# Reading the spectrum of h into both partition halves: one load with an outer dimension of two, or two loads of 64 rows

## The chip, the cores and the metric

The kernel runs on one core of one Trainium2 chip. The metric is device time in microseconds (us) of one execution; lower is better.

Names in the profile: PE is TensorE, PEld its weight loads, DVE is VectorE, ACT is ScalarE, POOL is GpSimd, SP is SyncE (which only issues transfers here). L307 is line 307 of the kernel. The change removes two lines, so line 307 of before is line 305 of after.

## The reference

Two layers in a row. The first, which matters here, is a long convolution by FFT:

```python
batch, seq, d_model = (8, 5696, 128)
L = 2 * S
Xf = np.fft.rfft(x, n=L, axis=1)        # x: 8 x 5696 x 128
Hf = np.fft.rfft(h, n=L, axis=0)        # h: 5696 x 128
Yf = Xf * Hf[None, :, :]
y = np.fft.irfft(Yf, n=L, axis=1)[:, :S, :]
# ... then a second layer: phases of y, two 5696 x 5696 token-mixing matrices, a channel mix
```

The second layer takes the last 1800 us and is not touched.

## The kernel before

The convolution is a two-level FFT done with matrix products. It works in eight groups: four pairs of batches times two halves of the channels. For each group there are four stages: A (first level), B (second level and the product with the spectrum of h), C and D (back). In stage B, TensorE makes a chunk of the spectrum of x in PSUM (`f2`); the 128 partitions are 64 rows of real parts and then 64 rows of imaginary parts. ScalarE copies the chunk to `xs`. VectorE multiplies `xs` twice, by the real and the imaginary plane of the spectrum of h. Both partition halves are multiplied by the same 64 rows, so the 64 rows of `hf_hbm[dh, c]` must be present twice, in partitions 0 to 63 and 64 to 127.

```python
fh = pool("fft_h", 4, conv, side="right")          # four buffers for hs
# ... cut ...
hf_hbm = nc.dram_tensor("hf_hbm", (2, 2 * NCK, N2, 2, HD * CK), F16, kind="Internal").ap()   # N2 = 64
# ... cut: h_chunk stores the spectrum of h, 24 stores ...
def stage_b(a_of, dh):
    def chunk(c):
        kh, c0, ck = CHK[c]
        hs = fh.tile([P, 2, HD * CK], F16, tag="hs", name="hs")
        hv = hs.rearrange("p r (d k) -> p r d k", k=CK)
        src = hf_hbm[dh, c]
        nc.sync.dma_start(hs.rearrange("p r n -> p (r n)"),
                          bass.AP(tensor=src.tensor, offset=src.offset,
                                  ap=[[0, 2], [2 * HD * CK, N2], [1, 2 * HD * CK]]))
        ps = f2(a_of, c)                                                   # TensorE
        xs = fs.tile([P, 2, HD, CK], F16, tag="xs", name="xs")
        nc.scalar.activation(xs[:, :, :, :ck], ps, AF.Copy)                # L304
        k0 = HALF[kh][0] + c0
        for r in range(2):
            nc.vector.tensor_tensor(                                       # L307
                uv[r][:, :, :, k0:k0 + ck], xs[:, :, :, :ck],
                hv[:, r:r + 1, :, :ck].to_broadcast([P, 2, HD, ck]), op=mult)
    return [lambda c=c: chunk(c) for c in range(2 * NCK)]                  # 12 chunks
# ... cut: stage C reads all of u_t and v_t (one buffer each) at L322 and L323 ...
    woven(stage_c(st), nxt, now)                     # stage C of this group, stage A of the next
    if dh == 0 and bp + 1 < B // 2:
        x16s[bp + 1] = load_x(bp + 1)                # 2.9 MB input load, by GpSimd, every second group
    # ... cut ...
    woven(stage_b(a_of, groups[g + 1][1]) if nxt else [], stage_d(st, bp, dh), now)
    # stage D ends with two stores of yt (712 KB each), on SyncE's queue like the hs loads
```

An hs load is 128 rows of 2 KB, 256 KB in all. The source pattern is written as "twice (step 0), 64 rows, 1024 elements".

Of the kernel before, what the change touches and what calls it, by code (L numbers as in the profile page):

```python
# [22 lines left out]
def kernel(  # L23
# [10 lines left out]
    nc = tc.nc  # L34
# [50 lines left out]
    N2 = 64  # L85
# [3 lines left out]
    CK = 8  # L89
    HD = D // 2  # L90
# [8 lines left out]
    hf_hbm = nc.dram_tensor("hf_hbm", (2, 2 * NCK, N2, 2, HD * CK), F16, kind="Internal").ap()  # L99
# [25 lines left out]
    for p0, p1 in ((0, 80), (80, NB)):  # L125
        nc.gpsimd.dma_start(u_t[p0:p1, :N2 * D],
                            bass.AP(tensor=h.tensor, offset=h.offset + p0 * N2 * D,
                                    ap=[[N2 * D, p1 - p0], [1, N2 * D]]))
# [79 lines left out]
    def f2(a_of, c):  # L208

        kh, c0, ck = CHK[c]  # L210
        a_, (k0, kn) = a_of[kh], HALF[kh]
        ps = psum()
        for j in range(ck):
            for ri in range(2):
                for e in range(2):
                    rows = slice(64 * e, 64 * e + 64)
                    nc.tensor.matmul(ps[:, e, j * HD:(j + 1) * HD],  # L217
                                     w_t2[rows, k0 + c0 + j, N2 * (1 - ri):N2 * (3 - ri)],
                                     a_[rows, ri * kn + c0 + j, :],
                                     start=(ri == 0), stop=(ri == 1))  # L220
        return ps[:, :, :ck * HD].rearrange("p e (k d) -> p e d k", k=ck)
# [70 lines left out]
    def stage_b(a_of, dh):  # L292

        def chunk(c):
            kh, c0, ck = CHK[c]
            hs = fh.tile([P, 2, HD * CK], F16, tag="hs", name="hs")
            hv = hs.rearrange("p r (d k) -> p r d k", k=CK)
            src = hf_hbm[dh, c]
            nc.sync.dma_start(hs.rearrange("p r n -> p (r n)"),
                              bass.AP(tensor=src.tensor, offset=src.offset,  # L300
                                      ap=[[0, 2], [2 * HD * CK, N2], [1, 2 * HD * CK]]))
            ps = f2(a_of, c)
            xs = fs.tile([P, 2, HD, CK], F16, tag="xs", name="xs")
            nc.scalar.activation(xs[:, :, :, :ck], ps, AF.Copy)  # L304
# [5 lines that stand above are left out]
        return [lambda c=c: chunk(c) for c in range(2 * NCK)]  # L310
# [211 lines left out]
    with tc.tile_pool(name="bpool", bufs=1, reuse_waits="tile") as bp, \  # L522
# [216 lines left out]
        for i, (k, p, tt, j0, s0, nj) in enumerate(stretches):  # L739
# [21 lines left out]
            if tt is None:  # L761
# [17 lines left out]
                if end_of_pair:  # L779
# [5 lines left out]
                    for h in range(2):  # L785
                        c, c0 = cs[h]
# [88 lines left out]
```

## Time and profile before

| | before |
|---|---|
| median time | 2571.7 us (2 runs) |
| span of the profiled run | 2567.6 us |
| eight stages B (end of one stage C to the first matmul of the next) | 53.3, 62.3, 50.2, 62.2, 49.4, 62.0, 49.5, 53.8; sum 442.7 us |
| eight stages C with A | sum 248.0 us |
| end of the last stage C to the end | 1801.2 us |

The 62 us stages are those beside an input load. The first is woven with the making of a table, and the last runs beside a load of 2.9 MB for the next part.

The waits view, lines chosen. Each line says who waited for whom: us in total, how many times, the longest.

```profile
engine line waited for: us in total, times, longest us
...
DVE u_t L307 <- DMA hs<-hf_hbm: 290.3, 64, 16.3
...
ACT xs L304 <- DVE v_t L307: 219.0, 51, 15.8
PEld L322 <- DVE u_t L307: 192.0, 8, 29.5
PE ps L322 <- DVE u_t L307: 190.8, 8, 29.3
```

Read it from the top as a chain: VectorE waits for hs, ScalarE waits for VectorE to free `xs`, TensorE waits (once per group, up to 29 us) for the last product before stage C can start. They are one wait seen three times, so they must not be added.

The timeline of a steady piece of a stage without an input load: start, duration, engine and line; in brackets, the idle time before and who ended it.

```profile
start us, us, engine line op out<-in xcount [idle before <-releaser]
272.81 20.66 SPq L299 DMA_DIRECT2D hs<-hf_hbm  x4
276.17 0.69 DVE L307 TENSOR_TENSOR u_t<-xs,hs 128x1024 f16<-128x1024 f16 x1 [4.25 <-DMA hs<-hf_hbm]
276.78 0.69 DVE L307 TENSOR_TENSOR v_t<-xs,hs 128x1024 f16<-128x1024 f16 x1
...
281.44 0.69 DVE L307 TENSOR_TENSOR u_t<-xs,hs 128x1024 f16<-128x1024 f16 x1 [3.98 <-DMA hs<-hf_hbm]
282.05 0.68 DVE L307 TENSOR_TENSOR v_t<-xs,hs 128x1024 f16<-128x1024 f16 x1
...
286.71 0.69 DVE L307 TENSOR_TENSOR u_t<-xs,hs 128x1024 f16<-128x1024 f16 x1 [3.98 <-DMA hs<-hf_hbm]
```

The products come 5.27 us apart (286.71 - 281.44), 1.3 us of work and 4 us of waiting. A period of 5.27 us for 256 KB is 50 GB/s. And SyncE is busy for 20.66 us with four issues: it is held back too. The tile view of hs gives all its loads of before: shortest, median and longest issue in ns, then the first and last start.

```profile
L299 SPq DMA_DIRECT2D hs<-hf_hbm x96: 482/5082/14242, 37.2 to 714.8; - x96
```

The first six issues, which come 1.2 to 23.7 us apart, take 0.52 to 0.62 us each; the 5.1 us are of issues that follow one another at once. So 5.1 us is not what such an issue costs by itself.

Three stretches with their busy times per engine: the stage B from 253.5 to 303.7 us (no input load), one beside an input load, and everything after the convolution.

```profile
core 0: us, PE busy (x) PEld busy (x) DVE busy (x) ACT busy (x) POOL busy (x), PEclk, DMA share, GB/s
...
159.80:222.10 62.30, 15.70 (x499) 14.43 (x497) 15.81 (x25) 17.07 (x20) 2.17 (x4) 0.62 0.33 83
253.50:303.70 50.20, 15.72 (x498) 14.47 (x496) 16.06 (x25) 17.06 (x20) 0.00 (x0) 0.63 0.13 46
...
766.50:2567.60 1801.10, 1684.78 (x8800) 807.59 (x8798) 1337.32 (x2590) 356.75 (x583) 793.97 (x1464) 0.96 0.83 157
```

In 50 us no engine works for more than 17.1 us, and the sixteen DMA engines together are 13% busy: 2 of 16 is 12.5%. The time hangs on a transfer, and the transfers use little of what there is.

### The profile page before, as it was taken

How to read it: one execution, taken by the hardware profiler on the slowest of the kernel's cores; microseconds unless marked ns; L12 is line 12 of the kernel's file. 1: busy time of each engine (PE TensorE's matmuls, PEld its weight loads, DVE VectorE, ACT ScalarE, POOL GpSimd, SP SyncE). 2: the span in 40 equal slices, each digit the busy share in tenths (PEclk: the TensorE clock that was granted, in tenths of full speed). 3: DMA queues.
4: the chain of work that ended last, by engine and by line, in shares of the span. 5: the costliest groups of instructions: out<-in, count | busy, mean ns of one | idle time of the engine just before them, and what ended most of it. 6: DMA issues, size and time to landing. Idle time of an engine off the chain costs nothing.

```text
span 2567.6 us, 42483 instructions
## 1 busy us (share of the span) xinstructions
PE 2090.9 (81%) x16255; PEld 1197.2 (47%) x16255; DVE 1695.1 (66%) x3004; ACT 637.8 (25%) x931; POOL 841.8 (33%) x1521
## 2 busy tenths in 40 slices
PE   4365446535745669999999999979999999999998
PEld 4365446525743424444444444433444444444444
DVE  5444435524563588888878876778777777777774
ACT  5432333324334522333323300000111111111111
POOL 3200000000002025444454566524445544455441
PEclk9687678767776689999999999999999999999998
DMA  5132231231338589999988999896778877888773
GB/s 119 51 74 62 69 76 61 69 97 42 103 97 197 158 228 171 177 172 174 171 149 166 174 174 143 137 267 109 138 138 153 144 135 138 140 153 138 139 135 66
DMA packets 406108, 340.45 MB, mean 133 GB/s; under 512 B 80879, under 2 KB 363375, under 8 KB 404079
## 3 DMA queue, kind: packets, MB, share of 16 engines
q0 software_dynamic: 218240, 143.00, 41.2%
q1 hardware_dynamic: 180560, 179.40, 23.5%
q10 hardware_dynamic: 7104, 15.34, 1.7%
q8 instruction: 127, 2.08, 0.3%
q14 instruction: 77, 0.63, 0.1%
HBM read 382.55 MB, written 97.93 MB: 187 GB/s over the span
## 4 chain that ended last, share of the span: by engine, by line
PE 55%; DMA 5%; DVE 3%; POOL 2%; issue 1%; ACT 1%; SPq 0%; DVEq 0%; ACTq 0%; POOLq 0%
PE m L814 50%; DMA wb<-in_moe_w_tok_r_dram 2%; POOL wb L536 1%; DMA wb<-in_moe_w_tok_i_dram 1%; DVE c L821 1%; PE utp L626 1%; PE v L633 1%; PE m L775 1%; PE m L777 1%; PE m L818 1%; DMA zr_hbm<-mag 1%; DVE wt L545 1%; DMA y_hbm<-yb 1%; PE theta_ps L377 0%; PE tpz L575 0%
## 5 line engine op out<-in xcount | busy, mean ns | idle before, releaser
L536 POOL DMA_DIRECT2D wb<-in_moe_w_tok_i_dram x720 | 390.0, 553 | 810.8 <-DVE wt L545 732.1
L536 POOL DMA_DIRECT2D wb<-in_moe_w_tok_r_dram x720 | 389.1, 555 | 397.8 <-DMA zr_hbm<-mag 277.3
L814 PE MATMUL m<-b,wt 128*128 128x512 bf16 x1936 | 455.1, 381 | 19.1 <-DVE wt L545 15.0
L545 DVE STREAM_TRANSPOSE wt<-wb 128x384 f32<-128x384 f32 (+2 forms) x720 | 360.1, 523 | 126.3 <-PE m L814 68.0
L814 PEld LDWEIGHTS <-wt 128*128 128x128 bf16 x1936 | 189.5, 98 | 254.3 <-DVE wt L545 18.2
L322 PE MATMUL ps<-r_u,u_t 128*128 128x128 f16 x1024 | 142.4, 231 | 191.7 <-DVE u_t L307 190.8
L821 DVE TENSOR_TENSOR c<-c,m 128x512 f32<-128x512 f32 x440 | 283.3, 669 | 0.0
L307 DVE TENSOR_TENSOR u_t<-xs,hs 128x1024 f16<-128x1024 f16 x96 | 64.2, 669 | 305.9 <-DMA hs<-hf_hbm 290.3
L628 ACT ACTIVATE uts<-utp 128x512 bf16<-128x512 bf16 (+1 forms) x90 | 53.3, 592 | 616.6 <-PE utp L626 616.6
L322 PEld LDWEIGHTS <-u_t 128*128 128x128 f16 x1024 | 111.5, 109 | 192.0 <-DVE u_t L307 192.0
L304 ACT ACTIVATE xs<-ps 128x1024 f16<-128x1024 f32 x96 | 92.1, 979 | 223.0 <-DVE v_t L307 219.0
L135 POOL DMA_DIRECT2D x<-in_x_dram x16 | 8.6, 542 | 419.3 <-PE ps L201 419.0
L201 PE MATMUL ps<-f_t,x 89*128 89x88 f16 (+1 forms) x1024 | 144.9, 302 | 0.8 <-DVE v_t L246 0.8
L323 PE MATMUL ps<-r_v,v_t 128*128 128x128 f16 x1024 | 139.7, 230 | 0.2
L201 PEld LDWEIGHTS <-x 89*128 89x128 f16 x1024 | 136.8, 269 | 1.1 <-issue 0.8
L623 ACT ACTIVATE ub<-c 128x512 bf16<-128x512 f32 (+1 forms) x90 | 56.4, 628 | 226.4 <-DMA wb<-in_moe_w_tok_i_dram 163.2
L323 PEld LDWEIGHTS <-v_t 128*128 128x128 f16 x1024 | 107.5, 105 | 3.0 <-issue 1.7
L217 PEld LDWEIGHTS <-w_t 64*128 64x128 f16 x3240 | 69.0, 108 | 72.7 <-issue 49.5
L577 ACT ACTIVATE yb<-tpz 128x512 bf16<-128x512 bf16 (+1 forms) x46 | 27.5, 597 | 168.5 <-PE tpz L575 132.2
L635 DVE SCALAR_TENSOR_TENSOR c<-v,c 128x512 f32<-128x512 f32 (+1 forms) x90 | 61.4, 682 | 10.8 <-PE v L633 8.6
L379 ACT ACTIVATE red<-theta_ps,magic 128x512 f32<-128x512 f32 (+1 forms) x46 | 31.6, 687 | 136.3 <-PE theta_ps L377 108.8
L307 DVE TENSOR_TENSOR v_t<-xs,hs 128x1024 f16<-128x1024 f16 x96 | 64.8, 675 | 0.0
(2848 smaller groups left out, 3845.3 us busy)
## 6 DMA issues: line engine op xcount, KB each, us to landing
wb<-in_moe_w_tok_r_dram POOLq DMA_DIRECT2D x352, 96.0 KB, 4.5
wb<-in_moe_w_tok_i_dram POOLq DMA_DIRECT2D x352, 96.0 KB, 4.9
wb<-in_moe_w_tok_r_dram POOLq DMA_DIRECT2D x352, 80.0 KB, 4.5
wb<-in_moe_w_tok_i_dram POOLq DMA_DIRECT2D x352, 80.0 KB, 3.9
hs<-hf_hbm SPq DMA_DIRECT2D x96, 256.0 KB
cp_hbm<-c SPq DMA_DIRECT2D x88, 256.0 KB
c<-cp_hbm SPq DMA_DIRECT2D x88, 256.0 KB
out_dram<-c SPq DMA_DIRECT2D x88, 256.0 KB
```

What stands on the lines that cost most here:

```text
L201: nc.tensor.matmul(ps[:, i // 4, (i % 4) * 2 * kn:(i % 4 + 1) * 2 * kn], lhs(q + i), f1_t[:NB, 2 * k0:2 * k0 + 2 * kn], start=True, stop=True)
L217: nc.tensor.matmul(ps[:, e, j * HD:(j + 1) * HD], w_t2[rows, k0 + c0 + j, N2 * (1 - ri):N2 * (3 - ri)], a_[rows, ri * kn + c0 + j, :], sta ...
L304: nc.scalar.activation(xs[:, :, :, :ck], ps, AF.Copy)
L307: nc.vector.tensor_tensor(uv[r][:, :, :, k0:k0 + ck], xs[:, :, :, :ck], hv[:, r:r + 1, :, :ck].to_broadcast([P, 2, HD, ck]), op=mult)
L322: nc.tensor.matmul(o, u_t[:, at:at + P], r_u, start=True, stop=False)
L323: nc.tensor.matmul(o, v_t[:, at:at + P], r_v, start=False, stop=True)
L536: nc.gpsimd.dma_start(wb[32 * i:32 * i + 32, :ng, :nj * 64], bass.AP(tensor=a.tensor, offset=a.offset + row0 * S + p * H + i * QR + j0 * 6 ...
L545: nc.vector.transpose(wt.rearrange("p j t r -> p (j t r)").bitcast(F32).rearrange("p (j g t) -> p g j t", j=TJ, g=4)[:, :ng, :nj], wb[:, : ...
L623: nc.scalar.activation(ub[:m].rearrange("p b d -> p (b d)"), c[:m], AF.Copy)
L635: nc.vector.scalar_tensor_tensor(c[:m], v[:m], 0.0, c[:m], op0=ALU.max, op1=ALU.add)
L814: nc.tensor.matmul(ms[q], a[q][:, j, :, r], bts[jj][q][:, r, :], start=(jj == 0 and r == 0), stop=(jj == NJ - 1 and r == 1 and q not in left))
L821: nc.vector.tensor_tensor(c, z, ms[q], op=op)
```

## The change

Each half is loaded by its own transfer. The bytes moved and the size of the rows stay. The intent is to get rid of the outer dimension of two.

```diff
-            src = hf_hbm[dh, c]
-            nc.sync.dma_start(hs.rearrange("p r n -> p (r n)"),
-                              bass.AP(tensor=src.tensor, offset=src.offset,
-                                      ap=[[0, 2], [2 * HD * CK, N2], [1, 2 * HD * CK]]))
+            for e in range(2):
+                nc.sync.dma_start(hs[64 * e:64 * e + 64], hf_hbm[dh, c])
```

## The prediction

> **What bounds it now.** The change touches only the convolution, the first ~790 of 2567.6 us. There stage B (multiply by the spectrum of h) runs eight times, between stages C+A. By the timeline (end of one stage C to the start of the next) the eight take about 53, 62, 50, 62, 50, 62, 50 and 54 us, 443 together. The waits view: VectorE waits 290.3 us for the hs load at L307, ScalarE 219 us for VectorE, TensorE 191 us at L322 for u_t (eight waits). Stage C needs all of u_t and v_t, one buffer each, so this is critical.
>
> In steady state a multiplication follows the last by 5.27 us, about 4 us of it waiting. 256 KB in 5.27 us is 50 GB/s. The packet records show hs packets of 2048 B, 85 ns each, about 25 per microsecond: two engines' worth of 16. SyncE's queue has 15824 four-byte completion packets; its 977 other transfers at 16 each leave 192 for the 96 hs loads: two each. The Trainium skill, "DMA: Bandwidth & Descriptors", section "Why a DMA increments its semaphore by 16 and not by 1", says why: the engine count is the largest up to 16 that divides the slowest dimension of both sides, here 2. SyncE is held 5.1 us per hs issue (median).
>
> **What the change does.** Same bytes and packets, 192 issues for 96, outermost dimension 64, so 16 engines. Estimate: 8 packets per engine x 85 ns = 0.7 us per chunk, four chunks prefetched. SyncE: 2 x ~0.5 us per chunk (64-row issues of L414 take 0.45 to 0.59 us). The page's "Rules for kernel authors" advises against splitting a transfer into partition halves, since halves share the engines; here the unsplit form has only two engines, so I expect that advice not to hold.
>
> **What then bounds stage B.** The first four chunks, prefetched today, already go at 1.45 to 1.49 us each. VectorE has 24 multiplications of 0.67 us = 16.2 us, ScalarE 12 copies of ~1 us and 7 stage-D copies of ~0.9 us = 17.6 us. Estimated, with start and tail:
> - three stages without an input load: ~21.5 instead of 50 us, 28.5 saved each;
> - three with one (16 KB packets of 1.23 us, alternating with hs packets for ~14 us, so the fifth chunk still waits): ~29 instead of 62, 33 saved each;
> - the first (e tables woven in) ~27 saved, the last (beside the ya load) ~29.
>
> Sum 3 x 28.5 + 3 x 33 + 27 + 29 = ~240 us, all critical. Less idle TensorE may mean less slow start in stage C (matmuls 0.31, then 0.22 us): a few us. Against: a changed instruction order; yt stores ahead of an hs load on the queue (1.4 MB, ~7 us). What follows the convolution only shifts.
>
> **Prediction.** 2335 us, 8 in 10 within 2300 to 2385. Faster by over 2%: 0.97; within 2%: 0.02; slower: 0.01.
>
> **What would show it.** VectorE's wait for hs falls from 290 to under 60 us, what remains being in the three stages with an x load. TensorE's wait at L322 falls below 60 us. hs issues fall from 5.1 to about 0.5 us, x192. Completion packets on that queue rise to 18704. Multiplications come ~1.5 us apart. L814 keeps its durations.
>
> **What would make it wrong.** A 64-row load still confined to few engines (no gain); yt stores queued ahead of each stage's twelfth load (~50 us less gain); x loads starving hs longer; a new order of the later phases costing or giving tens of us.

## More of the kernel before

The line of SyncE's queue on the page (packets, MB, share of the engines' time), for later:

```profile
q1 hardware_dynamic: 180560, 179.40, 23.5%
```

## The result

| | before | after |
|---|---|---|
| median time | 2571.7 us (2 runs) | 2329.16 us (2 runs) |
| ratio | | 0.9057, 95% interval 0.9018 to 0.9096 |
| span of the profiled run | 2567.6 | 2327.1 |
| stages B | 442.7 us | 24.1, 30.9, 20.7, 30.6, 20.6, 31.0, 19.8, 23.7; sum 201.4 us |
| stages C with A | 248.0 | 247.3 |
| after the last stage C | 1801.2 | 1801.8 |
| SyncE held per hs issue, median | 5.08 us (96) | 0.60 us (192) |
| four-byte completion packets on SyncE's queue | 15824 | 18704 |

Ratios are the mean time of one kernel's fast runs over that of the other's of the same rounds, so not quite the ratio of the medians quoted. The result is right to the reference.

The spans differ by 240.5 us and the sums of the stages B by 241.3 us: the whole gain is there. The order of the instructions of TensorE, VectorE, ScalarE and GpSimd, as the two traces record it, is the same in both kernels apart from buffer numbers; only SyncE's list differs. So nothing has to be explained by another order of the work on those engines. The second layer's matmuls (L814, L812 in after) keep a median of 379 ns.

The waits view after:

```profile
...
DVE u_t L305 <- DMA hs<-hf_hbm: 46.1, 13, 11.7
ACT xs L302 <- DVE v_t L305: 43.6, 21, 11.2
...
PE ps L320 <- DVE u_t L305: 32.7, 8, 6.9
```

The same chain is still there and much shorter: 46.1 us instead of 290.3. Asked stretch by stretch, 12.5, 12.3 and 12.6 us of it, 37.4 us together, lie in the three stages beside an input load.

The timeline of the like piece of the same stage (VectorE's lines, and the end):

```profile
...
205.54 0.69 DVE L305 TENSOR_TENSOR u_t<-xs,hs 128x1024 f16<-128x1024 f16 x1 [1.61 <-DMA hs<-hf_hbm]
206.15 0.68 DVE L305 TENSOR_TENSOR v_t<-xs,hs 128x1024 f16<-128x1024 f16 x1
206.75 0.68 DVE L305 TENSOR_TENSOR u_t<-xs,hs 128x1024 f16<-128x1024 f16 x1
...
208.00 0.69 DVE L305 TENSOR_TENSOR u_t<-xs,hs 128x1024 f16<-128x1024 f16 x1
...
213.27 0.29 PE L320 MATMUL ps<-r_u,u_t 128*128 128x128 f16 x1 [4.04 <-DVE u_t L305]
```

Products are now mostly 1.2 us apart (206.75 - 205.54), with a wait of 1 to 2 us here and there.

The stretches that answer to those shown of before, the hs issues and the queue:

```profile
...
131.20:162.10 30.90, 15.57 (x498) 14.24 (x497) 15.55 (x25) 16.73 (x20) 2.17 (x4) 0.78 0.82 175
192.50:213.30 20.80, 14.21 (x499) 12.88 (x498) 15.72 (x25) 16.69 (x20) 0.00 (x0) 0.92 0.42 118
...
525.30:2327.10 1801.80, 1683.15 (x8801) 807.43 (x8798) 1336.41 (x2590) 356.45 (x583) 793.82 (x1464) 0.96 0.83 156
```

```profile
L299 SPq DMA_DIRECT2D hs<-hf_hbm x192: 444/596/2650, 37.9 to 488.4; - x192
q1 hardware_dynamic: 183440, 179.41, 26.9%
```

The stage without an input load takes 20.8 us with ScalarE busy for 16.7 of it. The DMA engines are 42% busy there instead of 13%. The queue has 2880 packets more than before and the same bytes. These are completion packets: 192 loads of 16 engines each give 3072, 96 loads of two give 192, and 3072 - 192 = 2880. The two per load of before can also be measured: e9 below takes the hs loads off this queue, and 15632 four-byte packets remain there, 192 fewer than in before for 96 loads. The packet records agree: before never has more than four hs packets in flight at once, and two for most of the time; after has up to 16, now and then a few more.

### The profile page after: what moved, and what is told of

Its sections match the earlier page's. It is cut to its first block, busy times and chain, and to the rows that moved or that the text cites. A ratio compares the mean times of both kernels' runs of the same rounds, so it can differ in the third digit from the quotient of the medians.

```text
span 2327.1 us, 42585 instructions
## 1 busy us (share of the span) xinstructions
PE 2080.3 (89%) x16255; PEld 1187.5 (51%) x16255; DVE 1693.7 (73%) x3004; ACT 633.8 (27%) x931; POOL 842.6 (36%) x1521
## 4 chain that ended last, share of the span: by engine, by line
PE 62%; DMA 5%; DVE 4%; POOL 1%; issue 1%; ACT 1%; SPq 0%; DVEq 0%; ACTq 0%
PE m L812 56%; DMA wb<-in_moe_w_tok_r_dram 2%; POOL wb L534 1%; DVE c L819 1%; DMA wb<-in_moe_w_tok_i_dram 1%; DMA zr_hbm<-mag 1%; PE utp L624 1%; PE v L631 1%; PE m L773 1%; PE m L775 1%; PE m L816 1%; DVE wt L543 1%; DMA y_hbm<-yb 1%; DMA b<-zr_hbm 0%; PE theta_ps L375 0%
## 5 line engine op out<-in xcount | busy, mean ns | idle before, releaser
L812 PE MATMUL m<-b,wt 128*128 128x512 bf16 x1936 | 454.4, 381 | 19.6 <-DVE wt L543 15.6
L812 PEld LDWEIGHTS <-wt 128*128 128x128 bf16 x1936 | 189.3, 98 | 254.5 <-DVE wt L543 18.6
L626 ACT ACTIVATE uts<-utp 128x512 bf16<-128x512 bf16 (+1 forms) x90 | 53.3, 592 | 616.2 <-PE utp L624 616.2
L305 DVE TENSOR_TENSOR u_t<-xs,hs 128x1024 f16<-128x1024 f16 x96 | 63.9, 666 | 67.2 <-DMA hs<-hf_hbm 46.1
L575 ACT ACTIVATE yb<-tpz 128x512 bf16<-128x512 bf16 (+1 forms) x46 | 27.5, 597 | 166.2 <-PE tpz L573 133.1
L377 ACT ACTIVATE red<-theta_ps,magic 128x512 f32<-128x512 f32 (+1 forms) x46 | 31.6, 687 | 135.3 <-PE theta_ps L375 115.7
```

The lines of the kernel that those rows point to most:

```text
L305: nc.vector.tensor_tensor(uv[r][:, :, :, k0:k0 + ck], xs[:, :, :, :ck], hv[:, r:r + 1, :, :ck].to_broadcast([P, 2, HD, ck]), op=mult)
L812: nc.tensor.matmul(ms[q], a[q][:, j, :, r], bts[jj][q][:, r, :], start=(jj == 0 and r == 0), stop=(jj == NJ - 1 and r == 1 and q not in left))
```

## The experiments

The theory, "engines": the number of DMA engines that one transfer uses is set by its shape, two before and sixteen after. The Trainium skill, "DMA: Bandwidth & Descriptors", section "Why a DMA increments its semaphore by 16 and not by 1", gives the rule: the largest count up to 16 that divides the slowest dimension (of size above one) of both sides. Rivals: "splitting" (more, smaller transfers in flight are faster), "read twice" (a step of zero, or one transfer that reads a row twice, is slow), and "SyncE" (its 5 us per issue is the cause and not a consequence). The first four runs were to tell these apart; the rest ask what bounds the kernel after, and whether another form is better.

All stage lengths below are read as in the first table. Each time is a median with the ratio to the kernel before of the same rounds.

### e1_62_2: two transfers per half, of 62 and 2 rows

62 is 2 x 31, so the largest count up to 16 that divides it is 2.

```diff
             for e in range(2):
-                nc.sync.dma_start(hs[64 * e:64 * e + 64], hf_hbm[dh, c])
+                for r0, r1 in ((0, 62), (62, 64)):
+                    nc.sync.dma_start(hs[64 * e + r0:64 * e + r1], hf_hbm[dh, c, r0:r1])
```

> Each 64-row half of the kernel after is cut into 62 and 2 rows (four transfers a chunk, right result, no zero-step dimension). Theory, engines: 62 and 64-row sources share only the divisor 2 with an engine count up to 16, so each transfer runs on two engines, 64 packets of 85 ns on each per chunk = 5.4 us a chunk: the gain goes away, 2560 to 2600 us, VectorE waits for hs 280 to 310 us, completion packets of the SyncE queue 15632 + 384 x 2 = 16400. Rival, splitting: it is the separate transfers per half that help (more in flight, no row read twice within one transfer): stays at 2325 to 2360 us.

Measured: right result, 2597.0 us (2560 to 2600 stated), ratio 1.0113 (1.0098 to 1.0128). The whole gain is gone. 16400 completion packets, as expected, and products about 5.28 us apart as before. Its waits view:

```profile
DVE u_t L306 <- DMA hs<-hf_hbm: 318.5, 64, 16.7
...
PE ps L321 <- DVE u_t L306: 219.3, 8, 29.4
```

It is even about 29 us slower than before, and the wait is over the stated 310 us. In each of the last seven stages B the twelfth product comes 9.0 to 9.5 us after the eleventh instead of 5.3 to 6.0 us; these seven add up to 27.7 us more than in before. In SyncE's order the two yt stores stand after the load of the eleventh chunk, so ahead of the twelfth; in before and after they stand behind it. The packet records show the effect: in the third stage, 24 hs packets start in each us until they stop for about 3 us while yt packets are in flight, and the twelfth product comes after that. That is the danger that the prediction named ("yt stores queued ahead of each stage's twelfth load"): it did not strike the change itself, but it struck this variant. Splitting as such brings nothing: this kernel has twice the transfers of after, no step of zero, and no row read twice in one transfer.

### e2_61_3: halves of 61 and 3 rows

The same edit with 61 for 62.

> Halves cut into 61 and 3 rows. Engines: 61 is prime, so one engine carries 61 rows of each half and one of the 3: 124 packets of 85 ns = 10.5 us a chunk, twice before's. Twelve chunks then take 126 us, more than a stage B and the stage C after it together (81 to 93 us before): about 45 us more than before for each of eight stages, 2860 to 2980 us. Completion packets 15632 + 192 x 1 + 192 x 3 = 16400. Rival, splitting: 2325 to 2360 us.

Measured: right result, 2945.55 us, ratio 1.1474 (1.1457 to 1.1492), 16400 completion packets. Time and count are as stated. Stages B take 94.7 to 110.3 us; products are 10.22 us apart. Cutting off one row more than in e1 costs 349 us.

### e3_51_13: halves of 51 and 13 rows

The same edit with 51 for 62.

> Halves cut into 51 and 13 rows. Engines: 51 goes to 3 engines, 13 to 13, so the busiest has 36 packets = 3.05 us a chunk. Between before (5.27 us a chunk) and after (bound elsewhere at about 1.5 us): stage B odd about 29 us, even about 41, first and last about 32; 2390 to 2430 us. Completion packets 15632 + 192 x 3 + 192 x 13 = 18704, the same number as after. Rival, splitting: 2325 to 2360 us.

Measured: right result, 2452.23 us, ratio 0.9549 (0.9535 to 0.9563), 18704 completion packets. The time is outside the stated range. The mechanism is not: products are 2.97 us apart (3.05 stated). The miss is the yt stores again, which stand ahead of the twelfth load here too: the last product of seven stages comes 7.3 to 7.6 us after the one before, 31 us more in all than 2.97 us each. 2452 - 31 = 2421 would lie within 2390 to 2430.

Two neighbouring products each of e1, e2 and e3, in this order:

```profile
212.21 0.69 DVE L306 TENSOR_TENSOR u_t<-xs,hs 128x1024 f16<-128x1024 f16 x1 [4.04 <-DMA hs<-hf_hbm]
217.43 0.69 DVE L306 TENSOR_TENSOR u_t<-xs,hs 128x1024 f16<-128x1024 f16 x1 [3.93 <-DMA hs<-hf_hbm]
...
261.69 0.69 DVE L306 TENSOR_TENSOR u_t<-xs,hs 128x1024 f16<-128x1024 f16 x1 [9.14 <-DMA hs<-hf_hbm]
271.96 0.69 DVE L306 TENSOR_TENSOR u_t<-xs,hs 128x1024 f16<-128x1024 f16 x1 [8.98 <-DMA hs<-hf_hbm]
...
237.63 0.69 DVE L306 TENSOR_TENSOR u_t<-xs,hs 128x1024 f16<-128x1024 f16 x1 [1.92 <-DMA hs<-hf_hbm]
240.61 0.69 DVE L306 TENSOR_TENSOR u_t<-xs,hs 128x1024 f16<-128x1024 f16 x1 [1.69 <-DMA hs<-hf_hbm]
```

The three runs and before make one line. The counts of engines and packets are worked out from the rule, the times between products are means of the trace:

| rows per transfer | engines for the big one | packets on the busiest engine, per chunk | us between products | us per packet |
|---|---|---|---|---|
| 61 + 3 | 1 | 124 | 10.22 | 0.0824 |
| 2 x 64 in one (before) | 2 | 64 | 5.27 | 0.0823 |
| 62 + 2 | 2 | 64 | 5.28 | 0.0825 |
| 51 + 13 | 3 | 36 | 2.97 | 0.0825 |

The period is the packets of the busiest engine times 0.082 us, over a factor of 3.4. The packet records say the same: between 262 and 300 us of before, exactly two hs packets are in flight for 34.9 of 38 us; in e2 exactly one for 35.0 us of the same stretch.

### e4_one_transfer: one transfer, the two as the inner dimension

The result is wrong: row n goes to partitions 2n and 2n+1.

```diff
-            for e in range(2):
-                nc.sync.dma_start(hs[64 * e:64 * e + 64], hf_hbm[dh, c])
+            src = hf_hbm[dh, c]
+            nc.sync.dma_start(hs.rearrange("p r n -> p (r n)"),
+                              bass.AP(tensor=src.tensor, offset=src.offset,
+                                      ap=[[2 * HD * CK, N2], [0, 2], [1, 2 * HD * CK]]))
```

> Wrong result on purpose: one transfer a chunk as before, with the same zero-step dimension of two, but as the inner of the two row dimensions (64, then 2), so that each row lands in two neighbouring partitions instead of in both halves. Same bytes, same packets, 96 transfers. Engines: 16 engines, so as fast as after or a little faster (half the issues): 2315 to 2335 us, VectorE's wait for hs 35 to 60 us, completion packets 15632 + 96 x 16 = 17168. Rivals, splitting or the row read twice in one transfer: stays near before, 2540 to 2580 us.

Measured: 2325.24 us, ratio 0.9052 (0.9037 to 0.9067), 17168 completion packets. VectorE's line:

```profile
DVE u_t L307 <- DMA hs<-hf_hbm: 41.5, 9, 10.2
```

Only the order of two dimensions differs from before, and the whole gain is there, with 96 transfers, the step of zero and each row read twice in one transfer. That refutes "splitting" and "read twice".

### e5_stored_twice: one plain load of 128 rows

The right-result form of a single transfer: the spectrum is stored twice, and the load needs no trick.

```diff
-    hf_hbm = ... (2, 2 * NCK, N2, 2, HD * CK) ...
+    hf_hbm = ... (2, 2 * NCK, P, 2, HD * CK) ...
-            nc.sync.dma_start(
-                hf_hbm[:, c, :, ri, :].rearrange("h p n -> p h n"),
-                hst[kh][64 * ri:64 * ri + 64, c % NCK].rearrange("p h d k -> p h (d k)"))
+            for e in range(2):
+                nc.sync.dma_start(
+                    hf_hbm[:, c, 64 * e:64 * e + 64, ri, :].rearrange("h p n -> p h n"),
+                    hst[kh][64 * ri:64 * ri + 64, c % NCK].rearrange("p h d k -> p h (d k)"))
-            for e in range(2):
-                nc.sync.dma_start(hs[64 * e:64 * e + 64], hf_hbm[dh, c])
+            nc.sync.dma_start(hs, hf_hbm[dh, c])
```

> Right result: the spectrum of h is stored twice in memory (48 stores for 24 of half a KB-row kind), and each chunk is then one plain load of 128 rows. Engines: 128 divides by 16, so as fast as after: 2318 to 2335 us, completion packets of the SyncE queue 15632 + 24 x 16 + 96 x 16 = 17552; the extra stores (about 0.6 us of SyncE each, 14 us) lie in the time before the first stage B and are hidden. Rival, splitting (two loads are what helps): 2540 to 2580 us.

Measured: right result, 2325.37 us, ratio 0.9051 (0.9036 to 0.9066), 17552 completion packets. One load of 128 rows does as well as two of 64; the small lead over after is not clear of the intervals (0.9067 in the run a0_after below, in another set of rounds). The rows of the stores are of 1 KB, not of half a KB as the expectation has it. Whether the extra stores were wholly hidden is not shown: they keep SyncE until 75.1 us, and the first stage B takes 25.9 us and not 24.1.

### e9_pool_queue: before's load, issued from GpSimd

```diff
-            nc.sync.dma_start(hs.rearrange("p r n -> p (r n)"),
+            nc.gpsimd.dma_start(hs.rearrange("p r n -> p (r n)"),
```

> The kernel before, its single load with the leading dimension of two unchanged, issued from GpSimd and not from SyncE. The skill's page says that transfers from GpSimd that use few engines take them in turn from a cursor, where SyncE's take the lowest ones. If so, four loads in flight run on different pairs: 5.4 us of packets each, but one every 1.5 to 2 us; stages without an input load 22 to 30 us, 2350 to 2430 us. If the pair is always the same, as before: 2560 to 2600 us and 5.27 us between multiplications. If SyncE's 5.1 us per issue was the limit and not the engines, also fast, but then the packet records would show no more engines busy at a time.

Measured: right result, 2424.01 us, ratio 0.9438 (0.9424 to 0.9453). The time is within 2350 to 2430; stages without an input load take 29.8 to 31.0 us, at and a little over the end of the stated 22 to 30. The view of the tile hs:

```profile
L299 POOL DMA_DIRECT2D hs<-hf_hbm x96: 784/784/1182, 37.4 to 579.8; - x96
...
DMA to landing us min/median/max: 7.5/9.6/21.4
```

One load lands only 9.6 us after its issue (median), yet products come 2.5 us or so apart on average in the stages without an input load: up to four loads are in flight, one per buffer, and at times eight hs packets are in flight at once (in before they were two nearly all the time). That fits the statement of the Trainium skill, "DMA: Bandwidth & Descriptors", section "Why a DMA increments its semaphore by 16 and not by 1", that such transfers from GpSimd take their few engines in turn from a cursor. The records do not name the engine of a packet, so it is an inference. Note that the packets of this run are of 4 KB, as long as two rows, and take 0.160 us (median). Their size alone would not explain the gain: an estimate for one fixed pair of engines is 32 x 0.160 = 5.1 us per chunk, near the 5.27 of before.

### a0_after: the kernel after again

The base of the next three runs, in the same rounds. There is no edit.

> The kernel after again, beside the three variants of it: 2322 to 2332 us, VectorE waits for hs 44 to 48 us, eleven of the thirteen waits' time in the three stages with an x load.

Measured: 2328.49 us, ratio 0.9067 (0.9054 to 0.9079); VectorE waits 46.0 us for hs, 36.4 of them in the three stages with an input load (by five of 14 waits, where eleven thirteenths was stated); stages B 24.0, 30.9, 20.1, 31.0, 21.4, 31.0, 19.6, 24.0 us.

### e6_bufs6: six buffers for hs

```diff
-    fh = pool("fft_h", 4, conv, side="right")
+    fh = pool("fft_h", 6, conv, side="right")
     # and the pool w_small is closed right after its two uses (0.5 KB per partition),
     # since the six buffers missed the space by 0.3 KB
```

> The kernel after with six hs buffers for four (half a KB of space made by closing a small pool early). If the rest of the wait for hs comes from the input load's 16 KB packets, which hold each engine for 1.23 us between two hs packets, then two more prefetched chunks are multiplied while the input load lasts: the three stages with an input load 25 instead of 31 us, the others as they are; 2305 to 2318 us, VectorE's wait for hs 22 to 32 us. Rival, the rest of the wait is the issue rate of SyncE or the latency of a 64-row load: all eight stages would gain a little or none would.

Measured: right result, 2312.9 us, ratio 0.9003 (0.8989 to 0.9018): about 0.7% faster than after, with intervals that do not overlap. It is the fastest right kernel. The stages with an input load take 27.8, 27.5 and 28.3 us (25 stated), those without 18.9 (20.5 before it). So 9 of some 15 us saved in the stages B are where they were expected, less than stated, and the other stages gained too, where none was stated. The rival, by which all stages gain a little, is thus not ruled out for that part:

```profile
PE ps L322 <- DVE u_t L307: 31.2, 8, 6.9
DVE u_t L307 <- DMA hs<-hf_hbm: 28.9, 6, 9.3
```

### e7_x_pieces: the input load in four pieces

```diff
-                nc.gpsimd.dma_start(
-                    x16[p0:p1, e, :, :].rearrange("p n d -> p (n d)"),
-                    bass.AP(tensor=src.tensor, offset=src.offset + p0 * N2 * D,
-                            ap=[[N2 * D, p1 - p0], [1, N2 * D]]))
+                for n0 in range(0, N2, 16):
+                    nc.gpsimd.dma_start(
+                        x16[p0:p1, e, n0:n0 + 16, :].rearrange("p n d -> p (n d)"),
+                        bass.AP(tensor=src.tensor, offset=src.offset + (p0 * N2 + n0) * D,
+                                ap=[[N2 * D, p1 - p0], [1, 16 * D]]))
```

> The kernel after with each input row loaded in four pieces, so in packets of 4 KB for 16 KB, and nothing else. If the wait for hs is the turn-taking of packets, an hs packet then waits about 0.3 us and not 1.23 us: the fifth chunk lands some 3 us after its issue and not 10, stages with an input load 24 to 26 instead of 31 us; 2305 to 2320 us. The input load itself may last a little longer, without effect. Rival, the wait is for bandwidth (the input load takes all of it, whatever the packets): those stages stay at 31 us, 2325 to 2332 us.

Measured: right result, 2324.42 us, ratio 0.9053 (0.9041 to 0.9065), which is not clear of after's 0.9067. The expectation failed. The packets did become 4 KB (0.32 us each instead of 1.23), and the fifth product came 6.2 to 6.7 us after the fourth instead of 12 to 13. But then each of the next four came 2.3 to 3.9 us after the one before, and the stages ended after 29.7 to 30.8 us, as before. An estimate from the packets' times fits these: eight hs packets per engine with a 4 KB packet between each two take 8 x (0.084 + 0.324), about 3.3 us. By this reading, which is argued and not shown, the engines are shared while the input load lasts whatever the size of the turns. Smaller turns only let the hs chunks come one at a time and not four at once at its end, and the input load itself ends about 4 us later for it (24.1 to 25.3 instead of 19.9 to 20.7 us after the stage's start, by the packet records). The rival, that these stages wait for bandwidth, is nearer to the truth.

### e11_bufs6_x_pieces: both

The edits of e6 and e7 together.

> Both: six buffers and the input in pieces. Stages with an input load 21 to 23 us, near the 20.5 of those without; 2295 to 2308 us; VectorE's wait for hs under 15 us. It would be the fastest.

Measured: right result, 2313.75 us, ratio 0.9007 (0.8994 to 0.9019), the same as e6 alone. Stages with an input load take 27.3, 28.1 and 28.0 us and VectorE waits 25.1 us. The expectation (under 15 us of wait, 21 to 23 us for these stages) failed, as in e7: the seventh to the eleventh product each come 2.0 to 4.0 us after the one before.

### e8_quarters: four loads of 32 rows

The edit of e1 with 32 for 62.

> The kernel after with four loads of 32 rows a chunk, still 16 engines each. Same packets; four issues. At 0.5 to 0.6 us an issue SyncE needs 2.0 to 2.4 us a chunk, more than the 1.5 us that ScalarE needs: stages without an input load 23 to 27 us instead of 20.5, 2345 to 2375 us. If issues of few rows are shorter (0.22 to 0.3 us, as for 62 and 2 rows), no loss: 2322 to 2335 us. A yt store that the new order puts ahead of the twelfth load would add some 4 us for each of seven stages, about 30 us, as it did with halves cut in two.

Measured: right result, 2400.54 us, ratio 0.9342 (0.9324 to 0.936), 21776 completion packets (384 x 16 more than the other transfers'). Sixteen engines are used, and still 72 us are lost in the stages B (273.4 instead of 201.4 us). In the stages from the second on, the last product comes 7.3 to 8.8 us after the one before instead of 1.2 to 2.1, some 47 us in all: the order again puts yt ahead of the twelfth load, as SyncE's timeline of the second stage shows.

```profile
159.07 4.76 SPq L300 DMA_DIRECT2D hs<-hf_hbm  x9
163.94 1.13 SPq L345 DMA_DIRECT2D yt_hbm<-yt  x2
165.17 10.78 SPq L300 DMA_DIRECT2D hs<-hf_hbm  x12
```

The other 25 us go with products that are often 1.7 to 3.0 us apart; four issues at 0.42 us (median) are 1.7 us, over the 1.5 us that ScalarE needs for a chunk. That this is the cause of the 25 us is argued, not shown. The total lies in the slower of the stated cases (2345 to 2375 us, and about 30 more for yt), though an issue took less than the 0.5 to 0.6 us stated there and the wait behind yt took more than 30 us.

### e10_x_once: no input load beside stage B

Wrong: the first pair's input is used for all four.

```diff
-            x16s[bp + 1] = load_x(bp + 1)
+            x16s[bp + 1] = x16s[bp]
```

> Wrong result on purpose: the kernel after with the input loaded once and used for all four pairs, so no input load beside stage B. If the input load is all that sets those three stages apart, they take 20 to 21.5 us like the others: 3 x 10 us less, 2293 to 2303 us, and VectorE's wait for hs is under 12 us. If they stay above 25 us, something else in them is slower.

Measured: 2293.71 us, ratio 0.8931 (0.8916 to 0.8945). The three stages take 19.3, 19.9 and 19.8 us like the others, and VectorE's wait is:

```profile
DVE u_t L305 <- DMA hs<-hf_hbm: 9.9, 12, 2.2
```

So the input load is all that sets them apart. About 35 us of the kernel after are due to it (2328.5 - 2293.7, across two sets of rounds), and e6 gets back 16 of them at most.

## Why the prediction was right

The stated time was 2335 us in a range of 2300 to 2385; 2329.16 was measured. The mechanism is the one stated: a transfer confined to two engines, spread over sixteen. Term by term, in us saved per stage B:

| stages B | predicted | measured |
|---|---|---|
| first | 27 | 53.3 - 24.1 = 29.2 |
| three with an input load | 33 each | 31.4, 31.6, 31.0 |
| three without | 28.5 each | 29.5, 28.8, 29.7 |
| last | 29 | 53.8 - 23.7 = 30.1 |
| sum | about 240 | 241 |

That the sum agrees to 1 us is partly luck: the three stages with an input load saved 5 us less than stated, the other five together nearly 6 us more.

- **Two engines before, sixteen after: shown.** The completion packets were predicted at 18704 and are 18704. The counts of e1 to e5 also came out to the packet from the rule of the skill's page. e1 to e3 differ from each other only in where the halves are cut, and the time between products follows the count of engines; e4 gives the gain back by the order of two dimensions alone.
- **SyncE's 5.1 us per issue was a consequence: shown.** In e1 to e3 SyncE issues four transfers per chunk, and the period follows the packets of the busiest engine. In e4 one issue takes 0.51 us with as many loads as before, and the first six issues of before itself take 0.52 to 0.62 us.
- **What then bounds stage B: right.** Stages without an input load take 19.8 to 20.7 us (21.5 predicted), and 18.9 with six buffers, near ScalarE's predicted 17.6 us plus start and tail. (The first four chunks of before came 1.45 to 1.56 us apart on average, a little more than the 1.45 to 1.49 stated.)
- **The input load: right in kind, a little low.** The fifth product waits 12 to 13 us there, and those stages take 31 and not 29 us. The packets of the input load are in flight for 17.3 to 18.1 us, where an alternation of some 14 us was stated. e10 shows that the input load is the cause. What I thought about the turns of packets was too simple, as e7 showed: it decides which chunk waits, not how long the stage takes.
- **VectorE's remaining wait in the three stages: nearly.** 37.4 of 46.1 us are there; the other 8.7 us are short waits in the rest.
- **A few us from a faster start of stage C: not seen.** The sum of the stages C went from 248.0 to 247.3 us, although the granted clock in the stages B rose (0.63 to 0.92 in the stretches shown).
- **The two dangers that did not come.** The order of the other engines was unchanged, and the yt stores stayed behind the twelfth load. The second is luck: in e1, e2, e3 and e8, with four loads per chunk, they moved ahead of it, and where it was reckoned it cost 28 to 47 us (28 in e1, 31 in e3, 47 in e8).
- **The skill's advice against partition halves.** In the Trainium skill, "DMA: Bandwidth & Descriptors", the section "Rules for kernel authors" says of two transfers to disjoint halves "Don't bother — they serialize". Here they are worth 9.4%. The reason given is that both halves use all sixteen engines, so it holds only against a single transfer that does too. e5 is that transfer, and against it the halves indeed show no gain. Another row of the same table names exactly this case, a leading zero-step dimension that confines a transfer to few engines.

## What to carry to other kernels

Look at the outermost dimension of both sides of every transfer: if its size is not a multiple of 16, the transfer may run on few engines (here, by the rule that the counts and times of e1 to e3 bear out, 61 rows on one, 62 on two, 51 on three), and the tell-tale is a steady period with a low DMA share (here 13%, two of sixteen) while an engine waits for that load. Put the row dimension outermost, in one transfer or in two, and check the count of completion packets. After such a repair look at what now shares the engines: here it is the input load, and two more buffers of prefetch helped where smaller packets did not.

## What the Trainium skill lacked or had wrong

- "DMA: Bandwidth & Descriptors", "Rules for kernel authors": the row on two transfers to disjoint partition halves sets them against one 128-partition transfer, and is right there (e5: 0.9051 to after's 0.9067, no clear difference). What the row itself lacks is that a single transfer into 128 partitions can be on few engines by its shape; against such a one the halves gain (after to before: 0.9057).
- The same page, the rule for the number of engines: right in every case tried. Loads of 61, 62, 51, 13, 3, 2, 64, 32 and 128 rows gave completion counts of the queue (sums over all loads of a run) equal to those computed from 1, 2, 3, 13, 3, 2, 16, 16 and 16 engines. The page has a bandwidth per engine, but no time for one packet of 2 KB; here such a row takes 0.082 us in steady state, so two engines move 50 GB/s.
- The same page, "Queues, rings and completion order", says that an engine takes turns between queues by packets. The packets of a load from GpSimd with rows of 16 KB are 16 KB here, 1.23 us each, over the "≤4096 B preferably" of the page's section "SWDGE vs HWDGE vs iDMA"; hs packets of 2 KB on SyncE's queue wait for their turn meanwhile: in before, only 26 to 33 of them start in the 17.3 us in which the packets of an input load are in flight, against 24 in each us of the steady piece. No page warns that making them 4 KB does not help a kernel that needs both loads (e7: 2324.4 to 2328.5 us).
- No page puts a figure on how long a store that stands earlier on the same issuing engine's list delays the load behind it; here 1.4 MB of yt stores ahead of one hs load cost about 4 us in each of seven stages (e1).
